# Sliding-window attention and a token mixer on one core: even-odd q^T, a stepped score output, two operations split, a new order

## The chip, the cores and the metric

The kernel runs on one core of one Trainium2 chip. The metric is device time in microseconds; the time before is the median of three runs, 154.0 us (153.72 to 154.44). A core has TensorE (PE, with its weight loads PEld), VectorE (DVE), ScalarE (ACT), GpSimd (POOL) and SyncE (SP). In this kernel POOL issues the loads and SP the stores. Each engine works through its own queue in order and waits on semaphores for the others.

## The reference

Batch 8, 8 heads, 576 tokens, head width 64; all inputs and the output are fp32.

```
scores = (1/8) * q @ k^T                                  # per batch and head
rel    = pos_q - pos_k
scores = where(0 <= rel < 128, scores - 2^-(h+1) * |rel|, -1e9)
attn   = softmax(scores)
x      = (attn @ v), heads side by side                   # (8, 576, 512)
wq, wk = x @ w_q, x @ w_k                                 # (8, 576, 64)
mixed  = (1/8) * (wq @ wk^T) @ x                          # over tokens, per batch
out    = relu(mixed) @ w_out
```

## The kernel before, in words

Loads convert to fp16. Everything is unrolled over the eight batches. Work is cut into named operations, each bound to one engine when it is placed.

**Transposes.** For batches 1 to 7, q and k are loaded as `nat` tiles: two neighbouring tokens (j = 0, 1) of 128 token pairs in each partition, 256 tokens a load, plus a tail tile `ntl` of 64 tokens for both. TensorE transposes them (`tqk`, `tqkt`) into a PSUM bank, where all tokens of j = 0 stand ahead of those of j = 1. The eviction (`etqk`, `etqkt`; line 205 on ScalarE, 207 on VectorE, both in the helper `cp`) writes them to `qkT[batch % 4]` in token order: it reads PSUM with a step of 128 elements and writes without one. Four evictions of 128x1024 (`z0`, `z1`, each for q and k) and one of 128x512 are made per batch. Batch 0 is loaded with six tokens a partition (`six`), and its evictions are of 128x576.

**Attention.** For each batch and head pair (four pairs) two score operations `sc` (u = 0, 1; line 383) make ten small matmuls each: the k^T block of 64 keys is the stationary operand, 64 to 192 columns of q^T move. The results, keys by queries, go to a group of two PSUM banks, one for each head. `exp` on ScalarE (line 388) writes them to one of six `pt` buffers. `mul` on VectorE multiplies by the bias and mask table `bt`: first the edge blocks (line 401), then the whole (line 403). I call it the bias product. `pv` (line 421) multiplies by v with a column of ones; `nrm` takes the reciprocal (line 433) and multiplies (line 434) into `x`; `xt` transposes and `ext` evicts to `xT`.

**Mixing.** For each batch `wqk`, `wkt`, `g`, `mx` (lines 466 to 512) and their evictions `ewqk`, `ewq2` (to `wq`), `ewkt` (to `wkn`), `eg` (to `gm`), `emx` (to `rm`), then for each pair of batches nine output products `po` (line 533), evictions `eo` (to `osb`) and stores.

**What sets the order.** A table, `ORDER`, lists every operation once in the order in which it is emitted: its number, the letter of its engine (P, A, D, G, S), for TensorE the first PSUM bank, and `+n` for n idle products ahead of it. An idle product (`keep`, line 549) multiplies a tile of zeros, 128x512, and keeps TensorE at work while it waits. Each engine's queue is its operations in table order. Of software DMAs at most eight are under way: each waits for the eighth before it.

Of the kernel before, what the change touches and what calls it, by code (L numbers as in the profile page):

```python
# [26 lines left out]
31G 0D 2G 25G 36G 26G 24D 30G 3D 1D 15D 37G 20A 4D 28G 21A 51P7+13 38G 23A 29G 22A 16D 33G 18A 52D 34G 19A 17D  # L27
32G 49P7+7 6A 5A 35G 10A 11A 39G 50D 9A 45P6+3 7A 126G 12A 70P0 72P2 8A 47P7 44G 46D 40G 55P5+1 48D 41G 71A
57P4+1 56D 63P6 125G 73A 61P0 58D 53P5 129G 64A 13D 59P4 14D 42G 62A 60D 43G 74D 88P0+1 54A 90P2 141P7 128G
89A 81P4 65D 124G 91A 75P0 142A 127G 79P2 76D 82A 300G 66P6 92D 80A 77P1 27G 137P0 78A 67D 134G 93P2 138A  # L30
139P5 83D 131G 68P4 140A 133G 69A 94D 84P0 135P7 214G 85D 95P6 143P5 211G 136D 96A 86P4 144A 387G 163P0 154P2
216G 87A 156P6 164A 97P4 155A 147P0 132G 157A 174P2 99D 148A 130G 145P6 158D 98A 165P0 213G 146A 100P5 101D
215G 172P6 166A 102P5 175A 230P4 212G 103A 167D 173A 104P0 106P2 105A 108P6 231D 222P5 220G 107A 110P0 109A
217G 112P3 149D 111A 115P4 297G 223A 176D 168P0 221G 113A 159P6 116A 114S 218G 169D 150P2 117S 177P4 219G 160D
226P1 228P0 227A 301G 151D 161P7 229A 224P6 299G 178D 152P3 225A 118P2 162D 296G 179P5 153D 232P0 295G 180D
241P6 243P3 233A 170P5 119D 242A 259P0 171D 120S 121P2 244A 298G 250P6 260A 245D 261P4 305G 312P3 122A 181P0
262A 123S 385G 313D 251A 234P4 263D 182A 252P2 382G 246P6 235A 390G 253A 247D 310P5 184P4 183A 303G 264P2 236D
185A 248P7 311A 186P6 249A 308P5 304G 265D 187A 237P0 309A 192P2 188P6 238D 266P4 302G 193A 306P5 267A 254D
190P0 239P3 189A 386G 314P4 191D 307A 255P6 392G 315D 196P2 240A 343P0 256D 383G 318P4 199P3 344A 197A 316P6
389G 200D 194P0 198S 393P2 317A 195D 384G 201S 257P3 345P6 394D 205P1 391G 346A 208P0 319A 553G 258D 334P6  # L40
206A 209D 336P4 207S 268P2 335A 467G 210S 320D 337A 325P0 470G 327P6 269A 202P5 338D 326A 271P4 388G 270A
321P0 272D 328A 347D 339P2 273P4 203A 401P7 204S 340D 274A 471G 395P6 402A 279P4 322D 277P2 396A 472G 341P7
278D 323P1 397P0 342D 280A 348P2 324D 281P6 329D 275P4 469G 399P1 282A 276A 292P7 349D 398A 556G 330P4 400A
293D 289P6 331D 294S 468G 423P0 414P2 290D 405P4 424A 350P7 291S 332P6 473G 415A 351D 412P0 333D 479P7 413A
466G 432P2 480D 406A 283P6 554G 421P0 433A 555G 403P4 416D 564P7 422A 430P2 474G 565A 352P0 425D 558G 404A
485P7 284D 353A 481P5 286P4 486D 354A 285S 563G 482A 355P6 426P0 287A 356D 572P7 431A 475G 427D 288S 357P6
483P5 573A 559G 407D 428P4 417P0 484A 429D 408P2 418D 358A 365P4 363P6 476G 366A 364D 477P1 419P0 478A 409D
359P4 379P7 434D 360A 639G 410P6 420A 516P2 498P4 380A 411D 566P1 499A 642G 381S 570P0 567D 517A 435P6 557G
514P4 571A 496P2 436D 645G 376P1 497A 643G 437P0 515A 377D 487P6 489P2 500D 438A 562G 378S 505P4 488A 439P0
641G 518D 490A 361P6 637G 506A 501P2 491D 362A 519P4 440A 367P7 638G 502D 441A 442P6 368A 507P0 520D 640G  # L50
492P2 443A 369S 508A 568P7 646G 373P6 493D 569A 503P5 560G 509D 603P0 576P2 494P7 504A 647G 444P4 577A 654P5
644G 495D 374A 574P2 445D 604A 655D 561G 375S 594P6 370P4 575A 452P0 595A 648P5 453D 371A 450P2 448P6 649D
451A 510P0 372S 652P4 521P3 653A 463P2 449D 522A 511D 585P4 464A 583P6 656P3 586A 578D 465S 512P2 446P0 584A
601P4 513D 602A 592P6 447D 650P2 593A 523P4 605D 657A 457P7 651D 525A 460P6 524A 596D 458A 660P0 461A 667P2
459S 526P7 606P4 668A 587D 462S 454P6 527A 661A 597P2 607D 455A 588P0 598D 456S 528P7 687P4 589D 529A 685P2
608P6 688A 599P7 609D 534P0 686A 536P4 600D 590P6 535D 537A 579P2 591A 669P4 580D 658P0 547P7 670A 689D 659A
532P2 530P4 550P6 548A 533D 531A 549S 690P0 671D 551A 541P7 552S 678P2 691D 542A 676P4 581P6 677A 543S 538P7
582D 679A 662D 692P1 610P4 539A 693A 680D 540S 663P2 612A 672P0 611A 664D 681P6 613P5 544P4 673D 665P3 682D
614A 674P2 545A 615P5 675D 546S 683P4 666D 616A 684D 623P0 617P2 619P6 624D 618A 694P4 620A 621P0 695A 625P7
696D 697P6 628P5 622A 698D 626A 699P4 629A 627S 631P7 700A 630S 701P0 707P2 632D 703P4 634P6 702A 633S 708D  # L60
704A 705P0 635A 712P7 706A 636S 709P6 713D 715P5 714S 710D 718P4 711S 716A 721P7 717S 719A 720S 722A 723S
# [4 lines left out]
class Op:  # L66
    def __init__(self, name, engs, emit):
        self.name, self.engs, self.emit = name, engs, emit
        self.deps, self.ps_new, self.ps_read = set(), [], []
        self.eng = None  # L70
        self.pad = 0
# [11 lines left out]
class Plan:  # L83
# [28 lines left out]
    def run(self):  # L112
        order, done, bank = [], set(), [None] * 8
        for t in ORDER.split():
            t, _, pad = t.partition("+")
            k = t.rstrip("0123456789")
            o = self.ops[int(k[:-1])]
            o.eng, o.pad = ENGINES[k[-1]], int(pad or 0)
# [16 lines left out]
BOTH = ("ACT", "DVE")  # L135
NN = 3
# [11 lines left out]
def kernel(  # L148
# [24 lines left out]

    six = [pool.tile([96, H, 6 * D], F16, name=f"six{x}") for x in "qk"]
# [34 lines left out]
    def fill(e, o, x):  # L209
        if e == "DVE":  # L210
            nc.vector.memset(o, float(x))
# [9 lines left out]
    def load(name, dst, src, writes):  # L221
        plan.op(name, ("POOL",), lambda e: nc.gpsimd.dma_start(out=dst, in_=src), writes=writes)  # L222

    def setup():
# [30 lines left out]
        for n in range(NPT):  # L255
# [4 lines left out]
            plan.op("pfill", BOTH, pfill, reads=["wz", "wone"], writes=[("ptz", n), ("pt", n, 0), ("pt", n, 1)])  # L260
        for i in range(NV):
# [5 lines left out]
            plan.op("vfill", BOTH, vfill, reads=["wz", "wone"], writes=[("vones", i)])  # L267
# [25 lines left out]
    def load_v(b):  # L293
        vv = vn[b % NV]
        load("ldvt", vv[64:128, 4, :, 0:D], v[b, :, 512:576, :].transpose([1, 0, 2]),
             [("vn", b % NV, 4, hp) for hp in range(4)])
        if b == 0:
            for h in range(H):
                load("ldvh", vv[:, 0:4, h, 0:D], v[b, h, 0:512, :].rearrange("(t p) d -> p t d", p=P),
                     [("vn", b % NV, t, h) for t in range(4)])  # L300
        else:
            for t in range(4):
                load("ldv", vv[:, t, :, 0:D], v[b, :, 128 * t : 128 * t + 128, :].transpose([1, 0, 2]),
                     [("vn", b % NV, t, h) for h in range(H)])

    def transposes(b):
# [20 lines left out]
        for z in range(2):  # L327
            for x in range(2):
# [266 lines left out]
```

## Time and profile before

| | |
|---|---|
| median of the runs | 154.0 us (153.72 to 154.44) |
| the profiled execution's own time | 154.1 us |
| its span, first to last instruction | 152.3 us (1.8 us lie around it) |
| mean granted TensorE clock | 0.975 |
| TensorE busy / VectorE / ScalarE / GpSimd | 135.0 / 122.9 / 122.5 / 78.3 us |
| score matmuls | 640, in 64 operations |
| idle products | 26, 8.4 us busy |

Busy times are summed over the whole span. A mean duration of a matmul contains its way through the array, so the distance from one start to the next is what a matmul costs while TensorE is kept at work. "Idle before" names what ended the wait of the engine. PEclk is the granted clock, 1.00 being full speed.

### The profile page before, as it was taken

Reading aid. Unit: us, or ns where it says so; the run is one execution under the profiler, and the core shown is the slowest. Engines: PE = TensorE matmul, PEld = TensorE weight load, DVE = VectorE, ACT = ScalarE, POOL = GpSimd, SP = SyncE. Lnnn points to the kernel's source line nnn. Section 1 sums busy time; section 2 is a strip of 40 time slices with the busy share of each in tenths; the row PEclk is TensorE's granted clock in tenths of the full one; section 3 lists DMA queues with packets and bytes.
Section 4 is the critical chain, followed back from the end, with each engine's and each line's share of the span. In section 5 each row is a group of like instructions: output and inputs, shape, how many; then the busy total and the mean of one; then the engine's idle time right before and its main releaser. Section 6 shows DMA issues by size and latency. Waiting matters only on the chain.

```text
span 152.3 us, 5503 instructions
## 1 busy us (share of the span) xinstructions
PE 135.0 (89%) x2366; PEld 88.7 (58%) x2366; DVE 122.9 (81%) x213; ACT 122.5 (80%) x198; POOL 78.3 (51%) x102
## 2 busy tenths in 40 slices
PE   6786498877999899999999989799999999899990
PEld 2344287745776676567666867477666665664430
DVE  4836959858996999789989999999899999994330
ACT  7399866699769996799779979998899697837731
POOL 6999689687955876764479441996000000000000
PEclk9999956999999999999999999999999999999999
DMA  2999999999999999999999999999990503310564
GB/s 33 103 117 159 171 110 163 167 173 161 169 199 199 220 204 162 166 238 246 193 186 236 175 234 177 159 145 154 196 250 14 205 0 142 138 73 3 203 235 178
DMA packets 82535, 24.59 MB, mean 161 GB/s; under 512 B 75856, under 2 KB 77904, under 8 KB 82512
## 3 DMA queue, kind: packets, MB, share of 16 engines
q0 software_dynamic: 77328, 14.82, 120.2%
q1 hardware_dynamic: 5184, 9.44, 17.7%
q8 instruction: 18, 0.29, 0.8%
q14 instruction: 5, 0.04, 0.1%
HBM read 29.62 MB, written 9.44 MB: 256 GB/s over the span
## 4 chain that ended last, share of the span: by engine, by line
PE 44%; DVE 20%; ACT 16%; POOL 7%; issue 5%; DMA 5%; ACTq 0%; POOLq 0%; DVEq 0%
PE psb L533 16%; ACT pt L388 10%; PE psb L421 7%; PE psb L337 6%; DVE x L434 6%; DVE pt L403 6%; DMA natq<-in_q_dram 5%; PE psb L449 4%; PE psb L383 4%; DVE pt L401 3%; PE psb L512 3%; PE psb L496 2%; POOL vn L222 2%; POOL sixk L222 2%; POOL sixq L222 2%
## 5 line engine op out<-in xcount | busy, mean ns | idle before, releaser
L388 ACT ACTIVATE pt<-psb 128x768 f16<-128x768 f32 x64 | 49.4, 836 | 5.1 <-PE psb L383 4.8
L222 POOL DMA_DIRECT2D vn<-in_v_dram x44 | 36.6, 850 | 14.8 <-DMA vn<-in_v_dram 4.1
L533 PE MATMUL psb<-wout,rm 128*128 128x512 f16 x144 | 36.0, 380 | 0.3 <-DVE wq L207 0.2
L403 DVE TENSOR_TENSOR pt<-pt,bt 128x1536 f16<-128x1536 f16 x32 | 30.7, 959 | 1.1
L434 DVE TENSOR_TENSOR x<-psb,inv 128x640 f16<-128x640 f32 x32 | 26.4, 824 | 1.1
L205 ACT COPY qkT<-psb 128x1024 f16<-128x1024 f16 (+2 forms) x25 | 21.9, 894 | 3.7 <-PE psb L350 1.8
L421 PE MATMUL psb<-vn,pt 128*128 128x65 f16 x576 | 23.2, 198 | 1.7 <-DVE pt L403 1.4
L421 PEld LDWEIGHTS <-pt 128*128 128x128 f16 x576 | 20.8, 100 | 5.6 <-DVE pt L403 2.7
L383 PE MATMUL psb<-qkT 64*64 64x192 f16 (+2 forms) x640 | 19.7, 236 | 3.7 <-ACT pt L388 1.8
L207 DVE COPY qkT<-psb 128x1024 f16<-128x1024 f16 (+1 forms) x18 | 18.7, 1039 | 4.9 <-PE psb L316 4.1
L533 PEld LDWEIGHTS <-rm 128*128 128x128 f16 x144 | 12.4, 98 | 12.7 <-issue 0.9
L205 ACT COPY osb<-psb 128x512 f32<-128x512 f32 x26 | 15.5, 611 | 4.8 <-PE psb L533 4.4
L383 PEld LDWEIGHTS <-qkT 64*64 64x64 f16 x640 | 12.0, 107 | 12.0 <-issue 8.9
L519 ACT ACTIVATE rm<-psb 128x576 f16<-128x576 f32 x21 | 13.2, 683 | 3.1 <-PE psb L512 3.0
L401 DVE TENSOR_TENSOR pt<-pt,bt 64x512 f16<-64x512 f16 x32 | 13.5, 422 | 2.6 <-ACT pt L388 1.6
L222 POOL DMA_DIRECT2D natk<-in_k_dram x14 | 12.5, 899 | 5.1 <-DMA vn<-in_v_dram 4.0
L449 PE MATMUL psb<-idn,x 128*128 128x128 f16 x160 | 14.3, 223 | 0.3 <-DVE x L434 0.3
L222 POOL DMA_DIRECT2D natq<-in_q_dram x14 | 12.5, 895 | 2.3 <-DMA natq<-in_q_dram 0.8
L449 PEld LDWEIGHTS <-x 128*128 128x128 f16 x160 | 9.7, 99 | 4.5 <-DVE x L434 1.3
L207 DVE COPY osb<-psb 128x512 f32<-128x512 f32 x10 | 6.9, 688 | 5.1 <-PE psb L533 5.1
L205 ACT COPY xT<-psb 128x576 f16<-128x576 f16 x13 | 8.5, 656 | 2.7 <-PE psb L449 2.7
L337 PE MATMUL psb<-idn,natq 128*64 128x128 f16 x224 | 9.3, 228 | 1.5 <-DMA natq<-in_q_dram 1.2
(59 smaller groups left out, 166.6 us busy)
## 6 DMA issues: line engine op xcount, KB each, us to landing
out_dram<-osb SPq DMA_DIRECT2D x36, 256.0 KB, 4.4
natq<-in_q_dram POOLq DMA_DIRECT2D x14, 256.0 KB, 8.6
natk<-in_k_dram POOLq DMA_DIRECT2D x14, 256.0 KB, 8.2
vn<-in_v_dram POOLq DMA_DIRECT2D x28, 128.0 KB, 9.4
vn<-in_v_dram POOLq DMA_DIRECT2D x16, 64.0 KB, 7.2
sixk<-in_k_dram POOLq DMA_DIRECT2D x4, 144.0 KB, 4.9
sixq<-in_q_dram POOLq DMA_DIRECT2D x4, 144.0 KB, 4.9
wout<-in_moe_w_out_dram POOLq DMA_DIRECT2D x1, 512.0 KB, 7.6
```

What stands on the lines that cost most here:

```text
L205: nc.scalar.copy(o, i)
L207: nc.vector.tensor_copy(out=o, in_=i)
L222: plan.op(name, ("POOL",), lambda e: nc.gpsimd.dma_start(out=dst, in_=src), writes=writes)
L337: nc.tensor.transpose(o[64 * a : 64 * a + 64, y, j], w[:, 2 * y + a, j, :], idn)
L383: nc.tensor.matmul(ps32(g)[half : half + 64, o : o + w], T[r, 1, hp, k0 : k0 + 64], T[r, 0, hp, q0 : q0 + w], start=True, stop=True)
L388: nc.scalar.activation(out=blocks(pt)[:, :, 2 * u : 2 * u + 2, 0:192], in_=ps32(g).rearrange("t (a c) -> t a c", a=2)[:, :, 0:384].rearran ...
L401: nc.vector.tensor_tensor(out=d, in0=s, in1=w, op=ALU.mult)
L403: nc.vector.tensor_tensor(out=o, in0=o, in1=bt[:, 2 * hp : 2 * hp + 2, 0:192].unsqueeze(2).broadcast_to([P, 2, 4, 192]), op=ALU.mult)
L421: nc.tensor.matmul(ps32(g)[:, o : o + D + 1], pt[:, a, c : c + 128], vv[:, kb, 2 * hp + a, :], **flags)
L434: nc.vector.tensor_tensor(out=xb[:, :, 128 * hp : 128 * hp + 128].rearrange("t j (a d) -> t a j d", a=2), in0=px[:, :, :, 0:D], in1=iv.uns ...
L449: nc.tensor.transpose(ps16(g)[:, 128 * t : 128 * t + 128], xb[:, t, 128 * hp : 128 * hp + 128], idn)
L533: nc.tensor.matmul(ps32(g), rm[p % NR][:, db, o : o + 128], wout[:, db, :], start=(db == 0), stop=(db == 3))
```

## The change

1. **q^T in even-odd order.** For batches 1 to 7 the q half of `qkT` keeps the 288 even tokens ahead of the 288 odd ones. The eviction of a q block reads and writes runs of 128 elements. The k half stays in token order. The tail eviction becomes two instructions, one for q and one for k.
2. **Scores written in token order.** The moving operand of a score matmul is then two runs (even, odd) of half the columns, and its output is given a step of two words in PSUM, so that scores come out in token order as before. Batch 0 stays as it was.
3. **Own operations.** The edge product (`edge`) leaves `mul`, and the reciprocal (`rec`) leaves `nrm`: each has its own place in the table.
4. **Idle products in any bank.** `+n/b` names a bank b that is free at that point. There are 45 idle products in place of 26.
5. **New order.** The whole table is new: places, engines of evictions, banks, loads. Fills may now also go to POOL (none does), and v's loads into a buffer's first use come after its fill.

```diff
-31G 0D 2G 25G 36G 26G 24D 30G 3D 1D 15D 37G 20A 4D 28G 21A 51P7+13 38G 23A 29G 22A 16D 33G 18A 52D 34G 19A 17D
+24D 35G 0D 2G 34G 3D 324G 30G 33G 1D 18D 16A 28G 20D 26G 22A 4D 59P7+13/7 32G 21A 31G 57P6+3/6 29G 15D 23A 19D
...
                 def ev(e, z=z, x=x, g=g):
-                    cp(e, T[:, x, :, 256 * z : 256 * z + 256].rearrange("t y (p j) -> t y p j", j=2),
-                       ps16(g).rearrange("t (y j p) -> t y p j", y=4, j=2))
+                    if x == 0:
+                        cp(e, T[:, 0].rearrange("t y (j m) -> t y j m", j=2)[:, :, :, 128 * z : 128 * z + 128],
+                           ps16(g).rearrange("t (y j p) -> t y j p", y=4, j=2))
+                    else:
+                        cp(e, T[:, 1, :, 256 * z : 256 * z + 256].rearrange("t y (p j) -> t y p j", j=2),
+                           ps16(g).rearrange("t (y j p) -> t y p j", y=4, j=2))
...
-                    cp(e, T[:, :, :, 512:576], ps16(g)[:, 0:512].rearrange("t (y x c) -> t x y c", y=4, x=2))
+                    w = ps16(g)[:, 0:512].rearrange("t (y x c) -> t x y c", y=4, x=2)
+                    cp(e, T[:, 0].rearrange("t y (j m) -> t y j m", j=2)[:, :, :, 256:288],
+                       w[:, 0].rearrange("t y (m j) -> t y j m", j=2))
+                    cp(e, T[:, 1, :, 512:576], w[:, 1])
...
-                            nc.tensor.matmul(ps32(g)[half : half + 64, o : o + w],
-                                             T[r, 1, hp, k0 : k0 + 64], T[r, 0, hp, q0 : q0 + w],
-                                             start=True, stop=True)
+                            d, s = ps32(g)[half : half + 64, o : o + w], T[r, 0, hp]
+                            if b:
+                                d = d.rearrange("t (m j) -> t j m", j=2)
+                                s = s.rearrange("t (j m) -> t j m", j=2)[:, :, q0 // 2 : (q0 + w) // 2]
+                            else:
+                                s = s[:, q0 : q0 + w]
+                            nc.tensor.matmul(d, T[r, 1, hp, k0 : k0 + 64], s, start=True, stop=True)
...
-            plan.op("mul", ("DVE",), mu, reads=[("bt", 2 * hp), ("bt", 2 * hp + 1), ("be", 2 * hp), ("be", 2 * hp + 1)],
+            plan.op("edge", ("DVE",), edge, reads=[("be", 2 * hp), ("be", 2 * hp + 1), ("pt", n, 0), ("pt", n, 1)],
+                    writes=[("pte", n)])
+            plan.op("mul", ("DVE",), mu, reads=[("bt", 2 * hp), ("bt", 2 * hp + 1)],
                     writes=[("pt", n, 0), ("pt", n, 1)])
...
-        plan.op("nrm", ("DVE",), nrm, ps_read=[g], writes=[("xs", b % NX, hp)])
+        plan.op("rec", ("DVE",), rec, ps_read=[g], writes=[("inv", hp)])
+        plan.op("nrm", ("DVE",), nrm, ps_read=[g], reads=[("inv", hp)], writes=[("xs", b % NX, hp)])
...
-    def keep(g, n):
+    def keep(b, n):
         for _ in range(n):
-            nc.tensor.matmul(psb[:, g.bank, :], wz[:, 0:P], wz[:, 0:DM], start=True, stop=True)
+            nc.tensor.matmul(psb[:, b, :], wz[:, 0:P], wz[:, 0:DM], start=True, stop=True)
```

Three places of the order follow. POOL's loads behind the very first one, before: `sixk`, `sixq` are batch 0's k and q, `vn_81` its v, `natq_73` the first block of batch 1's q, `wqk` a mixing weight.

```order
L222 DMA wqk<-in_moe_w_q_dram 128x4x64
L222 DMA vn_81<-in_v_dram 64x8x64
L222 DMA wqk<-in_moe_w_k_dram 128x4x64
L222 DMA sixq<-in_q_dram 96x2x384
L222 DMA vn_81<-in_v_dram 128x4x64
L222 DMA sixq<-in_q_dram 96x2x384
L222 DMA vn_81<-in_v_dram 128x4x64
L222 DMA sixk<-in_k_dram 96x2x384 x2
L222 DMA sixq<-in_q_dram 96x2x384 x2
L222 DMA sixk<-in_k_dram 96x2x384
L222 DMA vn_81<-in_v_dram 128x4x64
L222 DMA natq_73<-in_q_dram 128x8x128
```

The same place now, from the third load on (the second is a `sixq`); `ntl_78` is batch 3's tail, `ntl_79` batch 1's.

```order
L232 DMA ntl_78<-in_k_dram 64x8x64
L232 DMA sixq<-in_q_dram 96x2x384
L232 DMA sixk<-in_k_dram 96x2x384
L232 DMA sixq<-in_q_dram 96x2x384
L232 DMA wqk<-in_moe_w_k_dram 128x4x64
L232 DMA sixq<-in_q_dram 96x2x384
L232 DMA sixk<-in_k_dram 96x2x384 x2
L232 DMA vn_81<-in_v_dram 128x4x64
L232 DMA ntl_79<-in_q_dram 64x8x64
L232 DMA vn_81<-in_v_dram 128x4x64 x3
L232 DMA vn_81<-in_v_dram 64x8x64
L232 DMA natq_73<-in_q_dram 128x8x128
```

Batch 0's q and k are all asked for by the tenth load instead of the thirteenth; batch 1's first q block is the 17th load instead of the 15th. The last load of batch 1's q and k is the 25th in both.

VectorE's queue around batch 0's first normalisations, before (`pt_88` to `pt_91` are the four head pairs' buffers, `inv` the reciprocals, `x_98` the normalised result):

```order
L433 RECIPROCAL inv_95<-psb 128x10
L434 TENSOR_TENSOR x_98<-psb,inv_95 128x2x5x64
L401 TENSOR_TENSOR pt_91<-pt_91,bt 64x2x4x64
L403 TENSOR_TENSOR pt_91<-pt_91,bt 128x2x4x192
L433 RECIPROCAL inv_94<-psb 128x10
L434 TENSOR_TENSOR x_98<-psb,inv_94 128x2x5x64
L401 TENSOR_TENSOR pt_90<-pt_90,bt 64x2x4x64
```

and now, with the tail of batch 1's q^T and k^T (`qkT_85`) at its end:

```order
L427 TENSOR_TENSOR pt_89<-pt_89,bt 128x2x4x192
L460 RECIPROCAL inv_97<-psb 128x10
L427 TENSOR_TENSOR pt_90<-pt_90,bt 128x2x4x192
L463 TENSOR_TENSOR x_98<-psb,inv_97 128x2x5x64
L427 TENSOR_TENSOR pt_88<-pt_88,bt 128x2x4x192
L460 RECIPROCAL inv_95<-psb 128x10
L463 TENSOR_TENSOR x_98<-psb,inv_95 128x2x5x64
L460 RECIPROCAL inv_94<-psb 128x10
L460 RECIPROCAL inv_96<-psb 128x10
L463 TENSOR_TENSOR x_98<-psb,inv_96 128x2x5x64
L215 COPY qkT_85<-psb 128x8x32
L215 COPY qkT_85<-psb 128x4x64
```

Bias products now stand between a reciprocal and its normalisation, and two of them behind the first reciprocal.

ScalarE's queue through batch 1's evictions, before (`xT_101` is batch 0's x^T):

```order
L205 COPY qkT_85<-psb 128x4x256
L388 ACTIVATE pt_90<-psb 128x2x2x192 x2
L205 COPY xT_101<-psb 128x576
L205 COPY qkT_85<-psb 128x4x256
L205 COPY qkT_85<-psb 128x8x64
L205 COPY xT_101<-psb 128x576 x2
L205 COPY qkT_85<-psb 128x4x256
L205 COPY xT_101<-psb 128x576
```

and now:

```order
L410 ACTIVATE pt_88<-psb 128x2x2x192
L213 COPY qkT_85<-psb 128x8x128 x2
L213 COPY qkT_85<-psb 128x4x256
L213 COPY xT_101<-psb 128x576
L213 COPY qkT_85<-psb 128x4x256
L213 COPY xT_101<-psb 128x576
L410 ACTIVATE pt_93<-psb 128x2x2x192
```

The q blocks are evicted as eight runs of 128 elements (128x8x128) where a k block has four of 256; ScalarE takes all four blocks of batch 1 instead of three, and batch 0's exponentials all come first.

More of the change, by code (lines that the diff above doesn't have):

```diff
@@ L70, in __init__ @@
         self.eng = None
-        self.pad = 0
+        self.pad = self.padbank = 0
 class Ps:
@@ L135 @@
 BOTH = ("ACT", "DVE")
+FILL = ("ACT", "DVE", "POOL")
 NN = 3
@@ L209, in fill @@
     def fill(e, o, x):
-        if e == "DVE":
+        if e == "POOL":
+            nc.gpsimd.memset(o, float(x))
+        elif e == "DVE":
             nc.vector.memset(o, float(x))
@@ L294, in load_v @@
         vv = vn[b % NV]
+        ones = [("vones", b % NV)] if b < NV else []
         load("ldvt", vv[64:128, 4, :, 0:D], v[b, :, 512:576, :].transpose([1, 0, 2]),
-             [("vn", b % NV, 4, hp) for hp in range(4)])
+             [("vn", b % NV, 4, hp) for hp in range(4)], ones)
         if b == 0:
@@ L299, in load_v @@
                 load("ldvh", vv[:, 0:4, h, 0:D], v[b, h, 0:512, :].rearrange("(t p) d -> p t d", p=P),
-                     [("vn", b % NV, t, h) for t in range(4)])
+                     [("vn", b % NV, t, h) for t in range(4)], ones)
         else:
@@ L303, in load_v @@
                 load("ldv", vv[:, t, :, 0:D], v[b, :, 128 * t : 128 * t + 128, :].transpose([1, 0, 2]),
-                     [("vn", b % NV, t, h) for h in range(H)])
+                     [("vn", b % NV, t, h) for h in range(H)], ones)
     def transposes(b):
@@ L561 @@
             if o.pad:
-                keep(o.ps_new[0], o.pad)
+                keep(o.padbank, o.pad)
             o.emit(o.eng)
```

112 lines of the change are left out of this document (60 added, 52 removed).

## The prediction

> **What bounds the kernel now.** I read the page first: its busy shares, then its chain. Each row names an engine with the microseconds it was busy, or with its share of the chain that ended last.
>
> ```profile
> span 152.3 us, 5503 instructions
> PE 135.0 (89%) x2366; PEld 88.7 (58%) x2366; DVE 122.9 (81%) x213; ACT 122.5 (80%) x198; POOL 78.3 (51%) x102
> PE 44%; DVE 20%; ACT 16%; POOL 7%; issue 5%; DMA 5%; ACTq 0%; POOLq 0%; DVEq 0%
> ```
>
> Three engines lie within ten points of each other and the chain passes among them, so the average names none. Next came the windows, cut by stage: the busy time of each engine in a stretch, then the granted clock.
>
> ```profile
> core 0: us, PE busy (x) PEld busy (x) DVE busy (x) ACT busy (x) POOL busy (x), PEclk, DMA share, GB/s
> 10.00:19.00 9.00, 5.10 (x138) 3.19 (x137) 6.44 (x13) 8.36 (x17) 7.63 (x11) 0.97 1.57 159
> 19.00:25.00 6.00, 6.00 (x100) 4.91 (x101) 4.17 (x8) 3.58 (x6) 5.46 (x7) 0.50 1.65 133
> 40.00:130.00 90.00, 86.00 (x1683) 59.33 (x1680) 83.44 (x139) 78.58 (x122) 44.42 (x54) 1.00 1.57 178
> 140.00:152.30 12.30, 8.47 (x50) 3.39 (x48) 2.92 (x5) 5.07 (x10) 0.00 (x0) 0.97 0.51 192
> ```
>
> From 40 to 130 us TensorE is busy 86.0 of 90 us and VectorE 83.4: the steady stage has 4.0 us of TensorE idleness left, and little else can be won there. The start is another matter: TensorE is busy 5.1 of 9 us, then works six microseconds at half clock. At the end only TensorE has much to do. The timeline shows what holds the start.
>
> ```profile
> 9.98 0.69 POOL L222 DMA_DIRECT2D sixk<-in_k_dram  x1
> 11.37 0.96 POOL L222 DMA_DIRECT2D natq<-in_q_dram  x1
> 18.98 1.06 PE L337 MATMUL psb<-idn,natq 128*64 128x128 f16 x16 [1.23 <-DMA natq<-in_q_dram]
> 21.11 0.88 POOL L222 DMA_DIRECT2D natk<-in_k_dram  x1
> 28.58 1.21 DVE L207 COPY qkT<-psb 128x1024 f16<-128x1024 f16 x1
> 29.85 0.68 PE L383 MATMUL psb<-qkT 64*64 64x192 f16 x28 [0.33 <-DVE qkT L207]
> natk<-in_k_dram POOLq DMA_DIRECT2D x1, 256.0 KB, 5.3
> ```
>
> Loads issued by POOL gate it, and batch 1's score products begin at 29.85 us behind a VectorE copy that queued until 28.58 us.
>
> **The change, part by part.** *Copies of q^T.* These rows give the mean ns of one eviction from PSUM.
>
> ```profile
> L205 ACT COPY qkT<-psb 128x1024 f16<-128x1024 f16 x17 | 17.3, 1034 | 1.8 <-PE psb L337 1.7
> L207 DVE COPY qkT<-psb 128x1024 f16<-128x1024 f16 x11 | 13.4, 1218 | 0.7 <-PE psb L337 0.6
> L205 ACT COPY xT<-psb 128x576 f16<-128x576 f16 x13 | 8.5, 656 | 2.7 <-PE psb L449 2.7
> L207 DVE COPY xT<-psb 128x576 f16<-128x576 f16 x19 | 8.1, 450 | 0.3 <-PE psb L449 0.2
> L207 DVE COPY qkT<-psb 128x576 f16<-128x576 f16 x7 | 5.3, 758 | 4.2 <-PE psb L316 4.1
> L205 ACT COPY qkT<-psb 128x512 f16<-128x512 f16 x7 | 4.1, 590 | 2.0 <-PE psb L350 1.8
> ```
>
> On VectorE the two strided copies (758 ns for 576 elements, 1218 for 1024) fit 166 ns plus 1.03 ns per element; the contiguous xT copy (450 for 576) leaves, with the same 166, 0.49 per element. So a q block read and written in runs should take 166 + 1024 x 0.49 = 0.67 us instead of 1.22. ScalarE's points (656 contiguous, 1034 strided) lie on one line of 0.84 ns per element: nothing to gain. In the new order VectorE takes 5 k blocks and 7 q blocks instead of 11 blocks: 5 x 1.22 + 7 x 0.67 - 13.4 = -2.6 us. Two tail copies move to it, each now two instructions (256 strided elements 0.43, 256 contiguous 0.29): +1.4. On ScalarE a split tail copy costs about 0.15 us more (two times 0.37 against 0.59).
>
> *Other evictions move between the two engines.*
>
> ```profile
> L521 DVE TENSOR_SCALAR rm<-psb 128x576 f16<-128x576 f32 x11 | 8.2, 749 | 0.4 <-PE psb L512 0.4
> L207 DVE COPY osb<-psb 128x512 f32<-128x512 f32 x10 | 6.9, 688 | 5.1 <-PE psb L533 5.1
> L207 DVE CAST wkn<-psb 128x320 f16<-128x320 f32 x4 | 1.9, 487 | 0.3 <-PE psb L484 0.3
> L207 DVE CAST wq<-psb 64x576 f16<-64x576 f32 x2 | 1.5, 751 | 3.3 <-PE psb L466 2.1 <-ACT wT L205 1.2
> L211 DVE MEMSET pt<- 64x320 uint32 x3 | 1.0, 325 | 0.0
> L211 DVE MEMSET pt<- 64x128 f16 x3 | 0.5, 165 | 0.2
> L207 DVE CAST gm<-psb 128x256 f16<-128x256 f32 x1 | 0.4, 416 | 0.0
> ```
>
> VectorE gains four osb copies (+2.75), five wq (+3.76), one rm (+0.75) and one gm (+0.42), and loses three wkn (-1.46). With the fills of two more pt buffers (2 x 0.49 = +1.0) and two of batch 0's 576-element copies fewer (-1.5) the whole comes to +4.5 us. The four osb copies are in the last batch pair's output, where VectorE was busy 2.9 of 12.3 us; one rm and one wq lie there too. Inside 40 to 130 us it is about +0.8 us: I take 0, between 0 and +2.3, as it has 6.6 us free there; if that cover is gone it lands in full.
>
> *Reciprocal and edge product as own operations.* The same instructions in another order. VectorE's queue now has a value product's reciprocal, then another head pair's bias product, then the normalisation. If the reciprocal waits for its value product, the bias products queued behind it wait too, and TensorE's next value products wait for those. I cost it at nothing; bounds -0.5 and +1 us, all in the start.
>
> *Score products with a step of two in PSUM.* Same columns, same order in a product; batches 1 to 7 make 56 products of ten matmuls whose output words now lie every second word, in two passes. No row of before shows a matmul writing so. Two neighbours bound it: a product between other work at full clock, and one at half clock. Columns: start, duration, engine.
>
> ```profile
> 78.97 0.36 PE L383 MATMUL psb<-qkT 64*64 64x64 f16 x10
> 79.29 0.64 PE L337 MATMUL psb<-idn,natk 128*64 128x128 f16 x16
> 79.86 0.36 PE L383 MATMUL psb<-qkT 64*64 64x64 f16 x10
> 80.15 0.60 PE L533 MATMUL psb<-wout,rm 128*128 128x512 f16 x2
> 19.98 0.53 PE L383 MATMUL psb<-qkT 64*64 64x64 f16 x10
> 20.44 1.18 PE L421 MATMUL psb<-vn,pt 128*128 128x65 f16 x18
> 84.49 0.86 PE psb L533 x4
> ```
>
> From its start to the next work's a product takes 0.29 us (79.86 to 80.15) at full clock and 0.46 (19.98 to 20.44) at half. So the price is between 0 (the step is free) and 0.17 us (words go out at half rate); a gain is excluded, since no column goes. I take 0.17. At full clock TensorE puts out 4 x 512 words per partition in 0.86 us, 2.4 per ns. The fastest stepped access to PSUM in any row is ScalarE's, 1 / 0.84 = 1.2 per ns, exactly half; and VectorE moves neighbours at twice the rate of stepped elements (0.49 against 1.03). The row nearest to a stepped output is thus the half-rate one, though ScalarE's line, alike for both layouts, speaks for a free step. 56 x 0.17 = 9.5 us.
>
> The Trainium skill, "Advanced Engine Details and Errata", section "PSUM Cachelines", says that PSUM is served in lines of two fp32 words and that a non-contiguous pattern slows matmuls significantly. It gives no figure. By it the sum is on the side of 9.5 us; by ScalarE's line alone it would be 0. No run here shows it yet.
>
> TensorE's 4.0 us of idleness between 40 and 130 us absorbs part: longer products fill its waits. I take all 4.0; at the other bound none, as half the chain's waits are elsewhere. It leaves +5.5.
>
> *Idle products.* 45 instead of 26, each 0.86 / 4 = 0.215 us at full clock. Thirteen of the new ones stand before the first three groups of batch 1's transposes, where TensorE waited 1.23 us for a load; one is added at the very start; five later cost at most 1.1 us. I take 0: they stand where the engine waits. If the load is already there, the thirteen cost 2.8 us.
>
> *Loads and the start.* Batch 0's last q or k load is three loads earlier in POOL's queue (about 2.1 us at 0.7 each) and the first natq two later (1.6 us). But the last load that batch 1's scores need is again POOL's 25th, so it lands as before at 21.11 + 5.3 = 26.4 us. Now all four blocks are evicted by ScalarE, which is free: 26.4 + 0.57 (transposes, 79.29 to 79.86) + 1.03 + 0.1 = 28.1, against 29.85: -1.7 us. Bounds: +1.0 (the later natq holds up the value products) and -3.3 (the six half-clock microseconds also go, half of them at most).
>
> The Trainium skill, "TensorE: Matmul & The Clock Gate", section "What's actually happening", ties full clock to a busy window of some 3.4 us. The trace agrees in kind: clock 0.50 right after the stretch with 5.1 of 9 us busy. By that rule the idle products would keep the clock, and the sum would lie nearer -3.3.
>
> Sum, against the profiled execution's own 154.1 us (0.1 above the median of 154.0): 154.1 - 1.7 + 9.5 - 4.0 = **157.9 us**.
>
> **The rivals.**
> *The step is free* (ends on the other side). Score products stay at 0.29 us. For it: ScalarE's one line. Then 154.1 - 1.7 = 152.4, own range 150.8 (with -3.3) to 153.6. It decides where the price falls below (4.0 + 1.7) / 56 = 0.10 us a product.
> *VectorE becomes the bound.* Step free, but its +2.3 us and the 1.1 us of idle products land in a stage where it has 6.6 us free, in pieces: 152.4 + 3.4 = 155.8. Against it: most of its added work is in the tail.
> *The copies do not get faster.* VectorE takes the rearranged q block one element at a time: 7 x 0.55 = 3.8 us more, half of it uncovered, step free: 154.3. Against it: the xT row.
>
> **How the numbers follow.** Half-rate step 0.50, free step 0.34, VectorE 0.09, copies 0.07. A difference under 0.5% (0.8 us) can't be told from none. Faster: 0.01 + 0.29 + 0 + 0.02 = 0.32; within: 0.03 + 0.04 + 0.01 + 0.03 = 0.11; slower: 0.46 + 0.01 + 0.08 + 0.02 = 0.57. The forecast's own range is 155.5 to 161.0: at the top half of the idleness absorbed and a third of the start's gain, 154.1 - 0.6 + 9.5 - 2.0. Since both signs hold chance, the range reaches down to the free step's end: 150.8 to 161.0; about 0.05 is left below and 0.1 above.
>
> **What would show each step.** Score products from start to the next work: 0.46 us, or 0.29 if the step is free, which would make the prediction wrong. VectorE's 128x1024 copies in two groups, 0.67 and 1.22 us. Batch 1's first score product near 28 us, and the clock from 19 to 25 us. TensorE's busy time from 40 to 130 us near 90 of 90, with ScalarE's exponentials waiting for score products more than now.

## The result, and the profile after

The changed kernel takes 158.7 us (median of 4, 158.58 to 159.03) against 154.06 (153.72 to 154.44) for the kernel before: a ratio of 1.030 [1.027, 1.033]. It is slower by 4.6 us. The forecast was 157.9.

The page of the changed kernel (profiled execution 158.81 us): span, busy time of each engine, and the shares of the chain that ended last.

```profile
span 157.0 us, 5536 instructions
PE 143.7 (92%) x2385; PEld 91.4 (58%) x2385; DVE 126.3 (80%) x228; ACT 116.6 (74%) x190; POOL 78.2 (50%) x102
PE 54%; DMA 14%; POOL 9%; DVE 9%; ACT 6%; issue 5%; POOLq 0%; ACTq 0%
```

TensorE is busy 8.7 us longer than before (143.7 against 135.0), and its share of the chain has gone from 44% to 54%; VectorE's and ScalarE's shares have shrunk, those of DMA (5% to 14%) and POOL (7% to 9%) have grown. The windows of the changed kernel, by stage (the columns are those of the windows of before: TensorE, its weight loads, VectorE, ScalarE, POOL, granted clock, DMA share, GB/s):

```profile
10.00:19.00 9.00, 7.67 (x168) 4.59 (x168) 6.58 (x14) 7.66 (x14) 8.24 (x11) 1.00 1.72 144
19.00:25.00 6.00, 4.80 (x98) 3.11 (x92) 3.76 (x7) 3.04 (x3) 5.58 (x8) 1.00 1.91 170
40.00:130.00 90.00, 87.25 (x1582) 58.48 (x1581) 79.64 (x137) 73.77 (x116) 43.86 (x53) 1.00 1.66 164
```

The half-clock stretch from 19 to 25 us is gone (clock 1.00 instead of 0.50), and TensorE does 98 matmuls there in 4.80 us where it did 100 in 6.00. From 40 to 130 us it is busy 87.25 of 90 us. The timeline of TensorE in the changed kernel (start, duration) shows a score product between other work, and batch 1's first four:

```profile
27.78 1.76 PE L407 MATMUL psb<-qkT 64*64 64x64 f16 x40
45.28 0.52 PE L407 MATMUL psb<-qkT 64*64 64x64 f16 x10
45.73 0.45 PE L479 MATMUL psb<-idn,x 128*128 128x128 f16 x5
46.11 0.52 PE L407 MATMUL psb<-qkT 64*64 64x64 f16 x10
46.56 0.45 PE L479 MATMUL psb<-idn,x 128*128 128x128 f16 x5
```

A score product takes 0.45 us from its start to the next work's (45.28 to 45.73, 46.11 to 46.56), where it took 0.29. Batch 1's scores begin at 27.78 us. In the kernel before, two matmuls of them ran at 29.30 us and the rest from 29.85, when VectorE's copy was done:

```profile
29.30 0.22 PE L383 MATMUL psb<-qkT 64*64 64x64 f16 x2
```

So the start gained 1.5 us by the first matmul, and 2.1 by the point that the forecast names. The groups of the changed kernel (count, busy us, mean ns of one, idle time before):

```profile
L407 PE MATMUL psb<-qkT 64*64 64x192 f16 (+2 forms) x640 | 27.8, 313 | 0.7 <-ACT wT L213 0.3
L213 ACT COPY qkT<-psb 128x1024 f16<-128x1024 f16 x16 | 16.3, 1018 | 5.8 <-PE psb L348 5.8
L215 DVE COPY qkT<-psb 128x1024 f16<-128x1024 f16 x12 | 10.9, 911 | 1.5 <-PE psb L348 1.2
L215 DVE COPY qkT<-psb 128x256 f16<-128x256 f16 x4 | 1.2, 349 | 0.0
```

VectorE's twelve 128x1024 copies are five k blocks and seven q blocks. With 1.22 us for a k block the q blocks come to (10.9 - 5 x 1.22) / 7 = 0.69 us; taken one by one they last 682 to 693 ns. ScalarE's copies stay where they were (1018 ns against 1034). Finally the waits of ScalarE's exponentials for score products, before and in the changed kernel (us in total, times, longest):

```profile
ACT pt L388 <- PE psb L383: 4.8, 7, 1.2
ACT pt L410 <- PE psb L407: 5.1, 12, 0.8
```

The wait is longer now, if not by much.

### The profile page after: what moved, and what is told of

It is laid out like the page before. It is cut to its first block, busy times and chain, and to the rows that moved or that the text cites. A ratio compares the mean times of both kernels' runs of the same rounds, so it can differ in the third digit from the quotient of the medians.

```text
span 157.0 us, 5536 instructions
## 1 busy us (share of the span) xinstructions
PE 143.7 (92%) x2385; PEld 91.4 (58%) x2385; DVE 126.3 (80%) x228; ACT 116.6 (74%) x190; POOL 78.2 (50%) x102
## 4 chain that ended last, share of the span: by engine, by line
PE 54%; DMA 14%; POOL 9%; DVE 9%; ACT 6%; issue 5%; POOLq 0%; ACTq 0%
PE psb L563 17%; PE psb L407 10%; PE psb L447 8%; PE psb L348 6%; DMA natk<-in_k_dram 5%; DMA vn<-in_v_dram 5%; PE psb L479 4%; PE psb L496 4%; POOL vn L232 4%; DMA sixk<-in_k_dram 4%; ACT pt L410 3%; DVE wq L215 2%; DVE x L463 2%; PE psb L526 2%; ACT wT L213 2%
## 5 line engine op out<-in xcount | busy, mean ns | idle before, releaser
L410 ACT ACTIVATE pt<-psb 128x768 f16<-128x768 f32 x64 | 48.9, 821 | 6.8 <-PE psb L407 5.1
L407 PE MATMUL psb<-qkT 64*64 64x192 f16 (+2 forms) x640 | 27.8, 313 | 0.7 <-ACT wT L213 0.3
L213 ACT COPY qkT<-psb 128x1024 f16<-128x1024 f16 (+2 forms) x29 | 21.3, 757 | 9.2 <-PE psb L348 5.8
L447 PE MATMUL psb<-vn,pt 128*128 128x65 f16 x576 | 22.3, 194 | 1.6 <-ACT pt L410 0.6
L407 PEld LDWEIGHTS <-qkT 64*64 64x64 f16 x640 | 15.7, 119 | 7.3 <-issue 4.2
L213 ACT COPY osb<-psb 128x512 f32<-128x512 f32 x22 | 12.9, 593 | 8.8 <-PE psb L563 5.0
L215 DVE COPY qkT<-psb 128x1024 f16<-128x1024 f16 (+2 forms) x21 | 15.9, 767 | 4.0 <-PE psb L327 2.5
L215 DVE COPY osb<-psb 128x512 f32<-128x512 f32 x14 | 9.7, 690 | 6.8 <-PE psb L563 4.9
L579 PE MATMUL psb<-wz 128*128 128x512 f16 x45 | 13.5, 418 | 1.6 <-DVE wz L235 1.3
L549 ACT ACTIVATE rm<-psb 128x576 f16<-128x576 f32 x20 | 12.6, 656 | 2.6 <-PE psb L542 2.6
```

Of the source, the lines that this page charges most:

```text
L213: nc.scalar.copy(o, i)
L215: nc.vector.tensor_copy(out=o, in_=i)
L407: nc.tensor.matmul(d, T[r, 1, hp, k0 : k0 + 64], s, start=True, stop=True)
L410: nc.scalar.activation(out=blocks(pt)[:, :, 2 * u : 2 * u + 2, 0:192], in_=ps32(g).rearrange("t (a c) -> t a c", a=2)[:, :, 0:384].rearran ...
L447: nc.tensor.matmul(ps32(g)[:, o : o + D + 1], pt[:, a, c : c + 128], vv[:, kb, 2 * hp + a, :], **flags)
L579: nc.tensor.matmul(psb[:, b, :], wz[:, 0:P], wz[:, 0:DM], start=True, stop=True)
```

## The experiments

Three questions: what does the stepped write cost, and why; what do the new order, the split operations and the idle products cost together; and what are the q copies worth? The theory of the forecast was that lone words leave TensorE at half rate and that the rest is free or helps. The rivals were that the two-run read costs the time, that the order does, or that the start does.

**no_step**: the changed kernel with its scores written in one run (the token order of the scores is left out).

```
-                                d = d.rearrange("t (m j) -> t j m", j=2)
```

> The changed kernel with one line less: the score matmuls of batches 1 to 7 write their output without a step, so that the even queries stand ahead of the odd ones within each matmul's columns and the bias table meets the wrong columns (part of the result that is left out: the token order of the scores). The moving operand is still two runs. Theory 'stepped output': a score product falls from 0.45 to 0.29 us from start to next work and the time to 152.4 us (150.8 to 153.6). Rival 'new order': the loss comes from the order, the idle products or VectorE's added work, and the time stays within 1.5 us of 158.7.

155.22 us (155.01 to 155.38), 1.011 [1.006, 1.016] of before. The page, one window and the score group of no_step:

```profile
PE 137.0 (89%) x2385; PEld 88.1 (57%) x2385; DVE 126.3 (82%) x228; ACT 116.2 (76%) x190; POOL 78.2 (51%) x102
40.00:130.00 90.00, 83.65 (x1635) 57.37 (x1634) 81.87 (x141) 75.92 (x120) 43.74 (x53) 1.00 1.63 170
L406 PE MATMUL psb<-qkT 64*64 64x192 f16 (+2 forms) x640 | 19.1, 234 | 2.0 <-ACT pt L409 0.9 <-ACT wT L213 0.5 <-ACT xT L213 0.3
```

The step is worth 158.70 - 155.22 = 3.5 us, and the score group goes from 27.8 back to 19.1 us. But the time does not fall to 152.4: without the step the changed kernel is still 1.4 us slower than the one before (0.9 to 2.4 by the interval). From 40 to 130 us TensorE idles 90 - 83.65 = 6.35 us, where before it idled 4.0.

**one_run_read**: the stepped write stays, but the moving operand is read as one run of q columns (which query meets which place is left out).

```
-  s = s.rearrange("t (j m) -> t j m", j=2)[:, :, q0 // 2 : (q0 + w) // 2]
+  s = s[:, q0 : q0 + w].rearrange("t (j m) -> t j m", j=2)
```

> The changed kernel with the stepped output kept, but the moving operand of a score matmul is one run of neighbouring columns instead of two (it takes the wrong queries; left out: which query a column is). Theory 'stepped output': nothing moves, 0.45 us a product and 158.7 us, within 0.5. Rival 'two-run read': it is the read in two passes that halves the rate; 0.29 us a product and about 152.4 us.

158.9 us (158.31 to 159.13), 1.034 [1.029, 1.040]: the time of the changed kernel. So the cost is that of the write. Alone this run cannot show that a read in two runs is free, as a slower read could hide behind the slow write. But no_step reads in two runs and writes in one, and its 640 score matmuls average 234 ns; in token_order_q, below, they read and write in one run, and average 234 ns too. Reading in two runs costs nothing that can be seen.

**exp_reorders**: the whole computation, but the scores go to PSUM as two contiguous planes (even queries, odd queries), and the exponential reads them interleaved.

```
-  d = d.rearrange("t (m j) -> t j m", j=2)
+  d = ps32(g)[half : half + 64, 512 * a : 512 * a + 384].rearrange(
+      "t (j m) -> t j m", j=2)[:, :, c // 2 : (c + w) // 2]
...
+  i = i.rearrange("t a (j k m) -> t a k m j", j=2, k=2)
```

> The changed kernel with the whole computation, in another layout: score matmuls write all even queries of a bank's 384 columns ahead of all odd ones (runs of 32 to 96 words without a step), and ScalarE's exponential reads them interleaved (a step of 192 words between neighbours) and writes token order. Theory 'stepped output', with ScalarE's reads alike for both layouts: 0.29 us a product, exponentials of 0.82 us as now, 152.4 us (150.8 to 153.6). If ScalarE pays for the interleaved read, its 56 exponentials lengthen by x each and the time by up to 56x. Rival 'new order': 157 us or more.

155.35 us (154.92 to 155.76), 1.011 [1.005, 1.017]: as no_step. Its exponentials in the groups:

```profile
L418 ACT ACTIVATE pt<-psb 128x768 f16<-128x768 f32 x64 | 48.8, 821 | 3.7 <-PE psb L408 2.6
```

One takes 821 ns, the mean that the changed kernel has with a contiguous read. Taking every next word from the other plane, 192 words on, costs ScalarE nothing. So the 3.5 us can be had back with the result unchanged.

**token_order_q**: the new order, the split operations and the idle products, with the q^T and the scores of the kernel before (evictions, tail and scores as there).

```
-                            if b:
+                            if False:
                                 d = d.rearrange("t (m j) -> t j m", j=2)
```

> The new order, split operations and idle products, with q^T, its evictions and the scores as they were in the kernel before (the whole computation). Theory 'stepped output': products of 0.29 us; VectorE's seven q blocks are back at 1.22 us (3.8 us more, half uncovered) and the tail copy is one instruction again, so 152.4 + 1.3 = 153.7 us (152 to 155). Rival 'new order': 157 us or more.

156.67 us (156.27 to 156.86), 1.020 [1.015, 1.025]. One window and two groups of it:

```profile
L400 PE MATMUL psb<-qkT 64*64 64x192 f16 (+2 forms) x640 | 19.4, 234 | 1.9 <-ACT pt L403 0.7 <-ACT wT L213 0.5 <-ACT xT L213 0.3
40.00:130.00 90.00, 83.35 (x1611) 57.12 (x1610) 83.98 (x139) 74.84 (x115) 43.38 (x53) 1.00 1.62 167
L215 DVE COPY qkT<-psb 128x1024 f16<-128x1024 f16 x12 | 14.6, 1220 | 1.0 <-PE psb L348 0.8
```

The order and what comes with it lose 156.67 - 153.82 = 2.85 us (2.3 to 3.9 by the interval). The idleness from 40 to 130 us is 6.65 us. The quicker q copies, with the split tail copies that come with them, gain 156.67 - 155.22 = 1.45 us in this order: all twelve blocks take 1220 ns here, which is 3.7 us of VectorE.

Where the order loses is plainer when the span is cut by work and not by time: at the end of batch 1's last score product, and at the end of the last score product of all. The rows show the stretch between these two points and the one behind the second, of the kernel before and then of token_order_q:

```profile
35.06:128.65 93.59, 89.09 (x1727) 61.28 (x1728) 86.57 (x143) 82.17 (x128) 48.63 (x59) 1.00 1.62 177
128.65:152.30 23.65, 19.09 (x187) 10.29 (x185) 12.74 (x24) 13.28 (x24) 0.00 (x0) 0.99 0.38 142
33.33:129.43 96.10, 88.32 (x1690) 60.49 (x1691) 89.84 (x148) 78.59 (x122) 49.29 (x60) 1.00 1.70 165
129.43:154.50 25.07, 20.78 (x211) 11.53 (x211) 16.59 (x28) 11.51 (x21) 0.00 (x0) 0.98 0.43 160
```

Batch 1's score products end 1.7 us earlier (33.33 against 35.06). The middle then takes 2.5 us longer though TensorE is busy 0.8 us less in it: it idles 7.8 us instead of 4.5. The end takes 1.4 us longer, because the new order leaves more to it: 18 more matmuls of value products and 8 more of output products. That part is the same 25.0 to 25.1 us in every profile of the new order but one (26.0 in rejoined, below), and 23.3 to 23.7 us in the four of the old order. The waits of TensorE between 40 and 130 us (total, times, longest) that differ most, first before, then in token_order_q:

```profile
PE psb L421 <- DVE pt L403: 0.4, 2, 0.2
PE psb L449 <- DVE x L434: 0.3, 1, 0.3
```

```profile
PE psb L472 <- DVE x L456: 1.3, 4, 0.6
PE psb L507 <- DVE wq L215: 0.9, 1, 0.9
PE psb L440 <- DVE pt L420: 0.8, 2, 0.4
```

Over all such waits of 0.2 us and more, TensorE waits 3.9 us for VectorE (its normalisations, wq copies and bias products) instead of 1.7. So most of what the middle lost is waiting for VectorE, read from one profile of each kernel.

**old_order_step** and **old_order_exp**: the order and operations of before, with q^T in even-odd order; once with the stepped write, once with planes and the interleaved exponential.

```
+                    if x == 0:
+                        cp(e, T[:, 0].rearrange("t y (j m) -> t y j m", j=2)[:, :, :, 128 * z : 128 * z + 128],
+                           ps16(g).rearrange("t (y j p) -> t y j p", y=4, j=2))
...
 old_order_step: +  d = d.rearrange("t (m j) -> t j m", j=2)
 old_order_exp:  +  d, i as in exp_reorders
```

> The kernel before, its own order, with the even-odd q^T and the stepped score output alone (the whole computation): no split operations, 26 idle products. Theory 'stepped output plus a weaker order': the step lands here on a fuller TensorE (4.0 us idle between 40 and 130 us), five VectorE q blocks gain 0.53 us each, so 154 + 9 - 4 - 1.4 = 157.6 us (156 to 159.5). Rival 'the new order is all of the loss, the step is absorbed': 154 us or less.

> The kernel before, its own order, with even-odd q^T and with score products written in runs and put in token order by the exponential's read (the whole computation). Both theories: no step, the old order, quicker q copies on VectorE (5 x 0.53 us), split tail copies on ScalarE (7 x 0.15 us): 152.5 us (151.5 to 153.5), faster than before. If the new order is worth something by itself, exp_reorders (155.4) would have beaten it.

old_order_step: 157.02 us (156.28 to 157.69), 1.022 [1.017, 1.026]. old_order_exp: 153.68 us (152.78 to 153.98), 1.000 [0.997, 1.003]. The score group and the middle window, of old_order_step and then of old_order_exp:

```profile
L396 PE MATMUL psb<-qkT 64*64 64x192 f16 (+2 forms) x640 | 26.8, 314 | 1.3 <-ACT pt L399 0.8 <-DVE qkT L207 0.5
40.00:130.00 90.00, 88.01 (x1617) 60.22 (x1614) 78.86 (x133) 76.28 (x122) 44.41 (x54) 1.00 1.53 171
```

```profile
L397 PE MATMUL psb<-qkT 64*64 64x192 f16 (+2 forms) x640 | 19.3, 237 | 2.5 <-ACT pt L407 1.8 <-ACT qkT L205 0.2 <-DVE qkT L207 0.2
40.00:130.00 90.00, 86.15 (x1684) 59.57 (x1681) 81.67 (x140) 79.16 (x128) 44.08 (x54) 1.00 1.54 179
```

The step costs 3.3 us in the old order as well (157.02 - 153.68), so it is not an effect of the order. And the quicker q copies with their split tail copies, worth 1.45 us in the new order, are worth nothing in the old one, where 152.5 us had been expected. Whether nothing waited for those copies there, or the split tail copies on ScalarE ate the gain, no run separates.

**few_idle**: exp_reorders without the 18 idle products ahead of batch 1's transposes and later.

```
-143P5+7/2 149P7+4/7 145P6+2/6 116P2+2/7 242P7+1/7 170P0+1/6 357P0+1/1
+143P5 149P7 145P6 116P2 242P7 170P0 357P0
```

> exp_reorders without the 18 idle products that stand after batch 0's score products (27 stay). Theory 'idle products keep the clock': the clock falls to 0.5 for some microseconds between 19 and 27 us as in the kernel before, and the time stays at 155.4 or rises by up to 1.5 us. Rival 'idle products are in the way': the clock holds, and the time falls by up to 1.1 us (the five late ones) to 3.9 us (all 18 at 0.215).

157.05 us (156.46 to 157.71), 1.023 [1.018, 1.027], 1.7 us more than exp_reorders. This run and those that follow come from other sets than exp_reorders, and from another chip; by the two ratios (1.023 and 1.011) the difference is 1.8 us. The same window of few_idle and of exp_reorders:

```profile
19.00:30.00 11.00, 8.53 (x168) 7.43 (x164) 7.50 (x15) 5.43 (x7) 9.32 (x13) 0.69 1.82 177
```

```profile
19.00:30.00 11.00, 8.18 (x185) 5.89 (x181) 7.34 (x15) 6.08 (x8) 9.46 (x13) 1.00 1.82 178
```

Without them the clock falls to 0.69 over these 11 us, as before it fell to half; with them it stays at 1.00. Batch 1's first score product begins at 29.04 us in few_idle, and between 27.3 and 28.3 in the eight profiles of the new order that have all 45. So the idle products do what they are there for, in this order.

**old_order_idle**: old_order_exp with more idle products at its start. The expectation counts 16; the edit adds 15, 41 in all.

```
-47P7 55P5+1 57P4+1 53P5 59P4 88P0+1 141P7
+47P7+2 55P5+3 57P4+3 53P5+1 59P4+1 88P0+2 141P7+6
```

> old_order_exp (153.7 us) with 16 more idle products at full clock between batch 0's score products and ahead of batch 1's first transposes (42 in all); the order of everything else is that of the kernel before. Theory 'idle products keep the clock': the clock stays at 1.00 from 19 to 30 us instead of 0.84, and as few_idle lost 1.7 us without them, the time falls to 152.0 to 153.0 us. Rival 'they stand in the way here': the clock holds, but batch 1's first transposes start later, and the time is 153.7 or more.

154.18 us (153.44 to 156.21), 1.000 [0.997, 1.003]: no gain. Two windows of old_order_exp, and of old_order_idle, each with batch 1's first score product:

```profile
19.00:30.00 11.00, 9.50 (x209) 7.66 (x204) 8.13 (x14) 7.72 (x12) 9.55 (x12) 0.84 1.63 147
30.00:40.00 10.00, 8.74 (x129) 5.66 (x127) 7.43 (x11) 9.45 (x16) 8.10 (x10) 0.83 2.09 169
28.40 0.56 PE L397 MATMUL psb<-qkT 64*64 64x64 f16 x22
```

```profile
19.00:30.00 11.00, 9.02 (x207) 6.66 (x205) 9.14 (x16) 7.86 (x13) 8.95 (x11) 1.00 1.52 142
30.00:40.00 10.00, 8.55 (x127) 5.74 (x128) 6.80 (x10) 9.60 (x16) 6.45 (x8) 0.83 2.23 163
29.22 0.56 PE L397 MATMUL psb<-qkT 64*64 64x64 f16 x22
```

The clock from 19 to 30 us goes from 0.84 to 1.00 and TensorE is busy half a microsecond less for about as many matmuls, yet the end does not move; a dip at 30 to 40 us stays. The rival fits: batch 1's first transposes begin at 19.96 us instead of 18.67, and its first score product 0.8 us later, which would mean that the added products took back what the full clock gained. Each figure is of one profile, and the first score product lies within 1.0 us from profile to profile in the new order, so this is not proven.

**wq_on_scalar**: exp_reorders with seven wq copies given from VectorE to ScalarE (engine letters alone).

```
-107D 199D 294D 481D 573D 668D 760D
+107A 199A 294A 481A 573A 668A 760A
```

> exp_reorders with the seven wq evictions that VectorE makes moved to ScalarE, at the same places of the table; nothing else. In exp_reorders TensorE waits 2.8 us before the wkt products for ScalarE's wT and VectorE's wq, which read the same banks. Theory 'the new order loses by this split': those waits shrink, VectorE is 5.2 us lighter, and the time falls to 153.5 to 154.5. Rival 'the loss is spread': within 0.5 us of 155.4, or slower since ScalarE is 4.4 us heavier.

154.84 us (154.34 to 155.7), 1.010 [1.007, 1.014]. That is 0.5 us less than exp_reorders, but against the kernel before, each in its own set, the two are alike (1.010 and 1.011). Two waits of TensorE in exp_reorders had pointed there:

```profile
PE psb L519 <- ACT wT L213: 1.0, 2, 0.7
PE psb L519 <- DVE wq L215: 0.9, 1, 0.9
```

These are 1.9 of the 2.8 us of the expectation; the other 0.9 lie before other products. In wq_on_scalar the wait for wq is gone and that for wT stays at 1.0 us. So a wait of 0.9 us was taken away and no gain can be told from none: the wq copies are not shown to be a part of the order's loss.

**rejoined**: exp_reorders with each edge product put back right ahead of its bias product, and each reciprocal right ahead of its normalisation, in VectorE's queue.

```
-98D 62A 87D 42G 99D
+98D 99D
...
+87D 88D
```

> exp_reorders (155.4 us) with each edge product put right ahead of its bias product and each reciprocal right ahead of its normalisation on VectorE, as in the kernel before; the rest of the new order stays. Theory 'splitting costs nothing': within 0.5 us of 155.4, a little slower if the interleaving was of use. Rival 'reciprocals that wait hold up the bias products behind them': the time falls by 0.5 to 1 us.

159.47 us (158.08 to 160.1), 1.033 [1.029, 1.038]: 4.1 us more than exp_reorders (3.5 by the two ratios), against every expectation. The window and a wait of TensorE's weight loads in rejoined, and the same wait in exp_reorders:

```profile
40.00:130.00 90.00, 82.48 (x1571) 56.49 (x1569) 80.46 (x137) 72.94 (x116) 43.50 (x53) 0.98 1.60 163
PEld L451 <- DVE pt L431: 5.6, 9, 1.3
```

```profile
PEld L452 <- DVE pt L432: 2.4, 4, 0.8
```

The weight loads of value products wait 5.6 us for bias products instead of 2.4, and TensorE idles 7.5 us from 40 to 130 us instead of 5.9. Where the pieces stand in VectorE's queue matters. In this order it helps that they are apart; nothing shows a cost of the splitting.

**step_sizes**: the changed kernel with four groups of eight idle products, whose results nothing reads, written in four ways: 256 columns in one run, 256 columns each second word, 256 columns as pairs of words with two words between pairs, and 128 columns each fourth word.

```
+        if n == 8 and b == 5:
+            w, d = 256, d[:, 0:256]
+        elif n == 8 and b == 2:
+            w, d = 256, d.rearrange("t (m j) -> t m j", j=2)[:, :, 0]
+        elif n == 8 and b == 7:
+            w, d = 256, d.rearrange("t (m j) -> t m j", j=4)[:, :, 0:2]
+        elif n == 8 and b == 6:
+            w, d = 128, d.rearrange("t (m j) -> t m j", j=4)[:, :, 0]
```

> The changed kernel, in which four groups of idle products at full clock are eight products each that write other patterns into their bank: 256 columns without a step, 256 at a step of two words, 256 as pairs of words with a gap of two, 128 at a step of four words. The distance from start to start is read from the timeline. Theory 'two neighbouring words go out at a time': 0.107, 0.213, 0.107 and 0.107 us. Rival 'any break in the run costs': pairs at 0.2 us as well. Rival 'a step is paid per word distance': 128 columns at four words take 0.2 us. The kernel's own time is not the point.

159.29 us in its profiled execution. The four groups in the timeline of step_sizes, in that order, all at full clock:

```profile
7.28 1.05 PE L587 MATMUL psb<-wz 128*128 128x256 f16 x8
...
15.93 1.89 PE L587 MATMUL psb<-wz 128*128 128x256 f16 x8 [0.17 <-ACT pt L409]
...
19.89 1.03 PE L587 MATMUL psb<-wz 128*128 128x256 f16 x8
...
21.67 1.05 PE L587 MATMUL psb<-wz 128*128 128x128 f16 x8
```

Eight products of 256 columns take 1.05 us in a run and 1.89 at each second word. As pairs with gaps they take 1.03, and half the columns at each fourth word take 1.05. So two neighbouring words go out in the time of one. A lone word costs as much as a pair, at both distances tried (two and four words), and gaps of two words between pairs cost nothing. The pairs began at even words; others were not tried. The Trainium skill, "Advanced Engine Details and Errata", section "PSUM Cachelines", says that every two consecutive elements should be contiguous for best throughput, which these four rows bear out; its sentence that any non-contiguous pattern slows a matmul goes too far, by the row of pairs.

## Why the prediction was right, and where it was not

The sign, the size (158.7 against 157.9) and the cause named for it, the half-rate write, are borne out. That the size is so near is partly luck, as two terms were wrong in ways that partly cancel: what the step adds came out at 3.5 us for 5.5, and all the rest at +1.4 (155.22 - 153.82) for -1.7.

- **Price of a stepped product: right.** 0.45 us from start to next work where 0.46 was forecast. The score group rose by 27.8 - 19.1 = 8.7 us against no_step, 0.155 a product; the forecast was 9.5 at 0.17. A product became 1.6 times as long and not twice, where eight products of 256 columns nearly doubled (1.05 to 1.89). The forecast took its price from a neighbour at half clock, 0.46 us, and that this fits so well is partly luck: what else bounds a product of ten small matmuls is not shown.
- **What idleness absorbs: right in kind and near in size.** Between 40 and 130 us the idleness fell from 6.35 us in no_step to 2.75, so 3.6 us were absorbed, against 4.0 forecast. TensorE was busy 87.25 of the 90 us, short of the "near 90" that was named as a sign. With all else TensorE's busy time rose by 6.7 us between the two profiles, not 8.7: the idle products' own time was 1.3 us shorter in the profile of after (13.5 us against 14.8), and 0.7 was not traced to a row. Its idleness fell from 16.6 to 13.3 us. What landed is 3.5 us, where 9.5 - 4.0 = 5.5 had been forecast.
- **The start, -1.7: the mechanism was right, the step from there to the end failed.** Batch 1's scores began at 27.78 us (28.1 forecast), and the clock held. The forecast's 29.85 us for the kernel before is the third matmul; the first ran at 29.30. In token_order_q, the order without the step, batch 1's last score product ended 1.7 us earlier than before; over the five profiles of the new order with all idle products and no step it is 0.7 to 1.7 us. None of it is left at the end, since the order loses 2.5 us in the middle and 1.4 at the end.
- **"The same instructions in another order" at nothing, VectorE's moved evictions at nothing: together this failed.** The new order with its splits, moved evictions and idle products costs 2.85 us in all, the gain of the start included. The loss lies in the middle and behind the last score product. In the middle TensorE waits longer for VectorE (3.9 us instead of 1.7); at the end it has 26 matmuls more to do. The bounds for the split had been -0.5 to +1 us, all in the start, and those for VectorE's evictions 0 to +2.3; the sum took 0 for both, and had no term for work that the order moves behind the last score product. VectorE's busy time itself rose by 3.4 us (126.3 against 122.9), less than the 4.5 forecast. As for causes, the later idle products are not it (1.7 us worse without them), the splitting is not shown to be (4.1 us worse rejoined), and moving the wq copies gave no gain that can be told from none. Which places of the new order make VectorE late stays open.
- **q copies: right.** 0.69 us for a q block on VectorE (0.67 forecast), nothing on ScalarE. What it would do for the whole time was not forecast except through the start; with the split tail copies it gains 1.45 us in the new order and none in the old one.
- **Idle products at nothing: right for where they stand.** They keep the clock at 1.00; without the later ones it is 0.69 from 19 to 30 us. The Trainium skill, "TensorE: Matmul & The Clock Gate", section "What's actually happening", has the clock follow how busy TensorE has lately been, and these rows agree. The further gain of up to 1.6 us that its rule left room for did not come: TensorE now waits 1.2 of the 6 us instead.

The whole in three differences of medians: the order with splits and idle products +2.85, the q copies -1.45, the stepped write +3.5. They add to +4.9 against 4.6 measured; the first two come from one shared set of runs, in which the kernel before took 153.82. The rivals fell as follows. The step is not free (8.7 us in its group). The copies did get faster. VectorE did not become the bound by its busy time: it has 10.4 us free from 40 to 130 us in the changed kernel (79.64 busy of 90). That others wait for it more than before is a matter of its order.

No version beat the kernel before: old_order_exp equals it, at 1.000 [0.997, 1.003].

## What to carry to other kernels

When a rearrangement has to be paid somewhere between TensorE, PSUM and the reader, don't let TensorE write lone words: write planes or pairs, and let ScalarE's read do the interleaving (821 ns either way here). Price a slower operation as its count times its price less the idle time around it, and read that idle time from the order in which it will run, not from the old one. A new order is a term of its own in the sum: this one started earlier and kept the full clock, and still cost 2.85 us. Cut the span by work (the end of one batch's score products, the end of the last), and not only by time, to see where a lead is lost.

## What the runs showed of the hardware

A matmul's output to PSUM goes out by pairs of neighbouring 4-byte words, as these times read: 1.05 us for eight products in runs, 1.89 at lone words, 1.03 as pairs with gaps, and for half the columns at each fourth word 1.05. A moving operand read in two runs costs nothing (234 ns a score matmul in no_step and in token_order_q). ScalarE reads PSUM interleaved over 192 words as fast as in a run (821 ns), while VectorE's copy of 1024 fp16 elements in each partition out of PSUM takes 1.22 us strided and 0.69 in runs.
